# Attention with a gated feed-forward branch on one core: accumulator gating, last additions and row scaling moved from VectorE to GpSimd, and 122 instead of 117 heads computed with V stationary

## The chip, the core and the metric

The kernel runs on one core of one Trainium2 chip. The metric is the device time of one execution in microseconds (us). The kernel before takes 1219.27 us (median of 3 runs, 1219.25 to 1219.4). The profile of one execution spans 1217.5 us from its first to its last instruction, with a granted TensorE clock of 1.000.

Engine names as the profile has them: PE is TensorE (matmuls), PEld its weight loads, DVE is VectorE, ACT is ScalarE, POOL is GpSimd, SP is SyncE, which issues most transfers. PSUM is the memory that matmuls write to, SBUF the working memory.

## What is computed

```python
# B=1, Sq=Sk=2048, D=512, H=32 heads of Dh=128, F=1792; inputs and outputs are bf16
xn = layernorm(x)
q  = (xn @ wq), split into 32 heads
p  = softmax(q @ k_cache^T * Dh**-0.5)          # per head
s  = concat_heads(p @ v_cache) @ wo
h  = relu(xn @ w1 + b1)**2
g  = silu(h @ w2 + b2)
out = x + s * g
```

## The kernel before, in words

**Tiling.** The 2048 query rows are cut into four blocks of 512 (index j), each of four row tiles of 128 (index qt; jt = 4*j + qt counts all 16). For each block the kernel runs over the 32 heads, so g = 32*j + h counts 128 (block, head) pairs, here called heads. Each head has eight steps; a step handles two key tiles of 128. Step numbers pi run from 0 to 1023 and are the clock of the program: the main loop at the end of the kernel emits, for each step, the scores of that step (`gen_scores`: two matmuls of 512 columns into `psA`, then one exponential of 128x1024 by ACT into one of eight `pT` buffers), some matmuls of other work from a job list (`fill_one`: query projections, the two feed-forward products, the output product with `wo`, all into the two banks of `psF`), and, two steps behind, the product with V (`gen_pv`).

**Two forms of the product with V.** In the A form (`gen_pv`) the probabilities are the stationary operand and V with a column of ones the moving one: eight matmuls of 129 columns a step, 64 a head. The ones column delivers the softmax denominator; DVE copies the result out (`o_un`, line 253), takes reciprocals (`rden`), POOL multiplies (`o_bf`), and a transposing transfer writes `oT`. In the B form (`gen_pv_b`) V is stationary and the probabilities move: two matmuls of 512 columns a step, 16 a head. The result is already transposed, ACT copies it to `o_col`, but the denominator has to be summed apart. For each of the eight `pT` tiles of a head, either DVE reduces the tile at once (`den_part`, line 286, `d_part<-pT`), or POOL first adds the two halves (`part_add`, line 239, `h_sum<-pT`) and DVE reduces the half (`part_half`, `d_part<-h_sum`). A few small DVE operations, two trips through memory (`den_sum` to `rec_read`) and one POOL multiplication (`den_scale`, `oT<-o_col,r_all`) follow. `at_a` chooses: heads below `FIRST_B` = 3, the last three, and those in `A_HEADS` = (10, 31, 41, 64, 96) take the A form, eleven in all; 117 take the B form.

**The gate and the output.** `job_o2` makes g: DVE adds the bias b2 to the product (`z_t`), ACT takes tanh of half of it, and DVE forms `g_all` = (tanh + 1) * z, which is twice silu. `job_wo` accumulates s in `acc`, eight heads (a chunk m) at a time, in f32. When all but the last chunk are in (line 1216 on), `acc_gate` multiplies `acc` by 0.5 * g_all on DVE (line 249), and `acc_add` adds x on POOL. When the last chunk comes, DVE multiplies it by 0.5 * g_all straight from PSUM into `tmp_t` (the same memory as `z_t`), adds `acc` into `out_t` (line 239), and the row tile is written out, by a transfer that POOL issues (line 294) or, in the last block, SP. In the last block the additions of row tiles 0 and 2 are POOL's.

**The next block's rows.** While block j runs, `ln_bn`, `ln_rstd` and `ln_next` normalise the x rows of block j+1. `ln_scale`, (x - mean) * rstd on 128x512 in bf16 by DVE (line 245, `xn_t<-x_ln`), is the first part of `ln_next`; a transposing transfer to `xnT` follows.

**What orders the work.** Nothing is scheduled at run time. The program is written out in advance by a planner that keeps for each engine the time at which it expects it to be free (`_cost` has the durations; `_uses_port` names the operations of DVE and POOL that the planner lets not overlap). Urgent work, such as copying a `psF` bank out, is emitted when its job ends. Work that can wait stands in lists: `quiet` for DVE (entered by `calm`, with a due step), `pool_quiet` for POOL, `sync_quiet` for SP. `fill_dve`, `fill_pool` and `fill_sync` take from them what is ready and fits before the expected time of PE plus some room (`ROOM` 800 ns for DVE, `POOL_ROOM` 300 ns for POOL). `fill_pool` also takes a `pT` tile over from DVE as a `part_add`, whenever POOL would be free and DVE's list is worth more than `POOL_OWED` = 3500 ns. So how many of the tiles POOL halves is an outcome of the planner, not a setting. On each engine the order then is fixed, and an instruction that waits holds up all behind it.

Of the kernel before, what the change touches and what calls it, by code (L numbers as in the profile page):

```python
# [5 lines left out]
ACT = mybir.ActivationFunctionType  # L6
# [53 lines left out]
def _cost(name, fn):  # L60
    f, k = fn.func, fn.keywords
    n = _elements(k["out"])
    if name == "PE":
        return n / 2.4 + 2.5, n / 2.4 + 166
    if name == "ACT":
        return n * 0.83 + 70, n * 0.83 + 172
    if name == "POOL":
        if f is _tt and n > 1:
            c = n * 2.3 + 55 if k["out"].tensor.name == "oT" else n * 2.05 + 60
            return c, c + 50  # L70
        return (500, 560) if f is _tt else (n + 100, n + 150)
    if f is _reduce_t:
        n = _elements(k["in_"])
    elif f is _reduce:
        n = _elements(k["in_"]) * 1.3 + 35
    elif f is _recip:
        n = n * 3.1
    elif f in (_bn_stats,):
        n = _elements(k["in_"])
    elif f is _ts and _in_sbuf(k["in0"]):  # L80
        n = n / 2
    return n / 0.96 + 70, n / 0.96 + 150


def _uses_port(name, fn):
    f, k = fn.func, fn.keywords
    if name == "POOL":
        return f in (_tt, _ts)
    if name == "DVE":
        if f in (_tt, _stt):  # L90
            return _in_sbuf(k["in0"]) and _in_sbuf(k["in1"])
        if f in (_ts, _copy):
            return _in_sbuf(k.get("in0", k.get("in_")))
    return False
# [206 lines left out]
def bass_recurrent_scan__mha_block_cached__dense_activation_squared_relu__prompt_kernel(  # L301
# [37 lines left out]
    LATE_EVICT = 250  # L339
    POOL_ROOM = 300  # L340
    SLACK = 1500
    FIRST_B = 3
    A_HEADS = (10, 31, 41, 64, 96)
    POOL_OWED = 3500
    HALF_SLACK = 600
    VW = 136
# [173 lines left out]
        ln_bn(j, i)  # L520
        ln_rstd(j, i)

    def ln_scale(j, i):
        jt = j * TPB + i
        assert jt < TPB or ln_prev(jt) in t_xnr
        t_xn[jt] = E(DV, partial(_ts, out=ln_y(jt), in0=ln_x(jt),
                                 scalar1=mv_t[:, i, 0:1], scalar2=rstd[:, i:i + 1],
                                 op0=ALU.subtract, op1=ALU.mult),
                     deps=[t_xr[jt], t_xnr.get(ln_prev(jt))])
# [7 lines left out]
        assert j < 2 or n_xuse[j - 2] == NFC + H  # L537

    def ln_next(j, i):
        ln_scale(j, i)  # L540
        ln_transpose(j, i)
        if i + 2 < TPB:
            ln_load(j, i + 2)
# [346 lines left out]
    def needs(fn):  # L890
        f, a = fn.func, fn.args
        if f in (den_part, part_half):
            m = b_no[a[0] // NPR]
            if m >= 2 and m - 2 not in t_sum:
                return None
            return [t_exp[a[0]]] if f is den_part else [t_part[a[0]]]
        if f in (den_sum, den_turn, den_write, den_read, den_total, den_recip, rec_write,
                 rec_read, den_scale):
            g = a[0]
            m = b_no[g]  # L900
            if f is den_sum and tiles[g] < NPR:
                return None
            first, before = {
                den_sum: (t_parts.get(g, []), t_row), den_turn: ([t_sum.get(m)], t_dw),
                den_write: ([t_row.get(m)], t_dr), den_read: ([t_dw.get(m)], t_tot),
                den_total: ([t_dr.get(m)], t_rw), den_recip: ([t_tot.get(m)], {}),
                rec_write: ([t_rec.get(m)], t_spr), rec_read: ([t_rw.get(m)], t_scale),
                den_scale: ([t_col.get(m), t_spr.get(m)], {})}[f]
            if m >= 2 and f not in (den_recip, den_scale):
                first = first + [before.get(m - 2)]  # L910
            return first
        if f is norm_recip:
            return t_oev[a[0]]
        if f is norm_scale:
            return [t_rden.get(a_no[a[0]])]
        if f is acc_gate:
            return [t_acc[a[1]], t_g.get(a[0] * TPB + a[1])]
        if f is acc_add:
            jt = a[0] * TPB + a[1]
            return [t_ug.get(jt), tok_xt.get(jt)]  # L920
        if f is ln_bn:
            return [t_xl.get(a[0] * TPB + a[1])]
        if f is ln_rstd:
            return [t_bn.get(a[0] * TPB + a[1])]
        if f is ln_next:
            return [t_xr.get(a[0] * TPB + a[1])]
        return gate_needs[fn]

    def ready_at(fn):
# [217 lines left out]
    def job_o2(j, qt):  # L1147
        jt = j * TPB + qt

        def mm(n, bank):  # L1150
            t = E(PE, partial(_mm, out=bankF(bank), lhsT=h2T[:, n, qt * P:(qt + 1) * P],
                              rhs=w2_sb[:, n, :], start=(n == 0), stop=(n == NFC - 1)),
                  deps=[tok_w2, t_bankF[bank], t_h2[j, n]], inc=(n == NFC - 1))
            if t is not None:
                assert n_w2[0] == NFC // 2
                t_o2[j, qt] = t
                t_o2j.append(jt)

        def evac(bank, step):
            s = jt % 2  # L1160
            assert jt < 1 or jt - 1 in t_g
            tz = E(DV, partial(_tt, out=z_t[:, s, :], in0=bankF(bank), in1=b2bc[:], op=ALU.add),
                   deps=[t_o2[j, qt], tok_b2, t_zrd[s], t_tmp[s]])
            box = [None]

            def gate():
                gs = jt % TPB
                t_g[jt] = t_zrd[s] = t_thr[0] = E(
                    DV, partial(_stt, out=g_all[:, gs, :], in0=th_t[:, 0, :], scalar=1.0,
                                in1=z_t[:, s, :], op0=ALU.add, op1=ALU.mult),  # L1170
                    deps=[box[0], t_fin.get(jt - TPB)])

            def tanh():
                box[0] = E(AC, partial(_act, out=th_t[:, 0, :], in_=z_t[:, s, :], func=ACT.Tanh,
                                       scale=0.5), deps=[tz, t_thr[0]])
                fn = partial(gate)
                gate_needs[fn] = [box[0]]
                calm(step + 8, fn)

            at(step + 1, tanh)  # L1180
            return tz
        return NFC, mm, evac

    t_fin = {}

    def job_wo(j, m, qt, c0=0, c1=D):
        jt = j * TPB + qt
# [15 lines left out]
        def evac(bank, step):  # L1203
# [2 lines left out]
                    t_wodone[j * H + h] = box[0]  # L1206
            place = (bankF(bank) if isinstance(bank, int) else bank[0])[:, 0:c1 - c0]
            if m == 0:
                t_acc[qt] = t = E(DV, partial(_copy, out=acc[:, qt, :], in_=place),
                                  deps=[box[0], t_fin.get(jt - TPB)])  # L1210
            elif not last:
# [1 line left out]
                                              in1=acc[:, qt, :], op=ALU.add),  # L1213
                                  deps=[box[0], t_acc[qt]])
            if m == len(CH[j]) - 2:
                calm(step + 16, partial(acc_gate, j, qt))
                pool_quiet.append(partial(acc_add, j, qt))
            if last:
                s = jt % 2
                assert all(x in t_g for x in t_o2j)  # L1220
                t = E(DV, partial(_stt, out=tmp_t[:, s, c0:c1], in0=place, scalar=0.5,
                                  in1=g_all[:, jt % TPB, c0:c1], op0=ALU.mult,
                                  op1=ALU.mult),
                      deps=[box[0], t_g[jt], t_tmp[s], t_zrd[s]])
                end = jt >= NQB * TPB - 2
                row = (x_t if end else out_t)[:, s, c0:c1]
                eng = GP if j == NQB - 1 and qt in (0, 2) else DV
                t_fin[jt] = t_tmp[s] = E(
                    eng, partial(_tt, out=row, in0=tmp_t[:, s, c0:c1],
                                 in1=acc[:, qt, c0:c1], op=ALU.add),  # L1230
                    deps=[t, t_u[jt], None if end else t_outdma[s]])
                eng, sl = (SP, sl_fin) if j == NQB - 1 else (GP, sl_out)
                dma = S.emit_dma(
                    eng, partial(_dma, out=out[0, jt * P:(jt + 1) * P, c0:c1],
                                 in_=row), sl[s], deps=[t_fin[jt]])
                if c1 == D:
                    t_outdma[s] = dma
            return t
        return nh, mm, evac

    def load_xt(jt):
        if jt < NQB * TPB:
# [3 lines left out]

    def acc_gate(j, qt):
        jt = j * TPB + qt
        t_ug[jt] = E(DV, partial(_stt, out=acc[:, qt, :], in0=acc[:, qt, :], scalar=0.5,
                                 in1=g_all[:, jt % TPB, :], op0=ALU.mult, op1=ALU.mult),  # L1250
                     deps=[t_acc[qt], t_g[jt]])


# [115 lines left out]
                                        in_=bass.AP(tensor=B_b2.tensor, offset=B_b2.offset,  # L1369
                                                    ap=[[0, P], [1, D]])), sl_b2)  # L1370

    at(62, load_b2)
    for i in range(2):
        at(140 + 8 * i, partial(load_xt, i))
    tok_w2 = None
# [14 lines left out]
    for j in range(NQB):  # L1390
        if j + 1 < NQB:
            for i in range(TPB):
# [2 lines left out]
                b = j * SPB + 8 * NPR + 4 * NPR * i  # L1395
                at(b, partial(calm, b + 32, partial(ln_bn, j + 1, i)))
                at(b, partial(calm, b + 32, partial(ln_rstd, j + 1, i)))
                at(b, partial(calm, b + 32, partial(ln_next, j + 1, i)))


    HD = D // 2
# [149 lines left out]
```

The softmax here doesn't subtract the row's maximum and nothing guards it: scores larger than these inputs give would overflow.

## Time and profile before

| | us | share of the span |
|---|---|---|
| span | 1217.5 | |
| PE busy | 1206.4 | 99% |
| ACT busy | 1090.4 | 90% |
| DVE busy | 1067.2 | 88% |
| POOL busy | 1064.2 | 87% |
| POOL `h_sum<-pT`, 758 of 1167 ns | 863.0 | |
| DVE `d_part<-h_sum`, 758 of 678 ns | 495.2 | |
| DVE `d_part<-pT`, 178 of 1213 ns | 215.4 | |
| PE, A form, 704 matmuls | 54.0 | |
| POOL `oT<-o_col,r_all`, 117 of 1284 ns | 150.2 | |

The page names for each group of instructions its line, engine, operation, output and inputs, how many there were, their busy time, the mean ns of one and the idle time of the engine just before them. Most operations are recorded at a shared helper's line (226 is a matmul, 239 an operation on two tensors, 249 one on two tensors and a scalar), so the tile's name tells them apart. A busy PE is no proof that it runs at its peak, since matmuls overlap: the records of two matmuls of 512 columns take 0.59 us together, though the second begins 0.22 us after the first. The distance from the start of one to the start of the next is therefore the measure. Some matmul records are missing from the trace, which shows as a distance of exactly twice the usual.

### The profile page before, as it was taken

How to read it: one execution, taken by the hardware profiler on the slowest of the kernel's cores; microseconds unless marked ns; L12 is line 12 of the kernel's file. 1: busy time of each engine (PE TensorE's matmuls, PEld its weight loads, DVE VectorE, ACT ScalarE, POOL GpSimd, SP SyncE). 2: the span in 40 equal slices, each digit the busy share in tenths (PEclk: the TensorE clock that was granted, in tenths of full speed). 3: DMA queues.
4: the chain of work that ended last, by engine and by line, in shares of the span. 5: the costliest groups of instructions: out<-in, count | busy, mean ns of one | idle time of the engine just before them, and what ended most of it. 6: DMA issues, size and time to landing. Idle time of an engine off the chain costs nothing.

```text
span 1217.5 us, 19712 instructions
## 1 busy us (share of the span) xinstructions
PE 1206.4 (99%) x6150; PEld 668.3 (55%) x6269; DVE 1067.2 (88%) x1865; ACT 1090.4 (90%) x1162; POOL 1064.2 (87%) x982
## 2 busy tenths in 40 slices
PE   9999999999999999999999999999999999999999
PEld 7555555555555555555555555555555555555556
DVE  4798889899999898879999999888999999889973
ACT  7898989999899898999989999999999999989995
POOL 1687999999898899999888899999998889999981
PEclk9999999999999999999999999999999999999999
DMA  9889888888778786777787777877778777677781
GB/s 209 182 202 211 193 181 168 187 170 184 179 157 178 170 161 155 164 159 153 169 167 159 171 167 166 163 163 164 163 163 167 164 164 164 158 160 164 160 156 49
DMA packets 510009, 203.47 MB, mean 167 GB/s; under 512 B 421808, under 2 KB 493744, under 8 KB 509904
## 3 DMA queue, kind: packets, MB, share of 16 engines
q1 hardware_dynamic: 507808, 198.13, 76.2%
q0 software_dynamic: 1424, 3.81, 1.1%
q8 instruction: 50, 0.82, 0.3%
q14 instruction: 55, 0.45, 0.1%
q10 hardware_dynamic: 672, 0.26, 0.1%
HBM read 128.23 MB, written 4.25 MB: 109 GB/s over the span
## 4 chain that ended last, share of the span: by engine, by line
PE 95%; DVE 3%; issue 1%; POOL 1%; ACT 0%; ACTq 0%; POOLq 0%
PE psA L226 36%; PE psO L226 32%; PE psF L226 24%; PE psO L231 3%; DVE d_part L286 1%; DVE acc L249 1%; POOL h_sum L239 0%; ACT pT L235 0%; PE psA L231 0%; DVE qt_sb L253 0%; DVE acc L239 0%; DVE d_sum L282 0%; PE psF L270 0%; POOL oT L239 0%; POOL acc L239 0%
## 5 line engine op out<-in xcount | busy, mean ns | idle before, releaser
L235 ACT ACTIVATE pT<-psA 128x1024 bf16<-128x1024 f32 x1025 | 1036.6, 1025 | 108.2 <-PE psA L226 71.2
L239 POOL TENSOR_TENSOR h_sum<-pT 128x512 f32<-128x512 bf16 x758 | 863.0, 1167 | 63.3 <-DVE d_part L286 31.0
L226 PE MATMUL psA<-qt_sb,kT 128*128 128x512 bf16 x1983 | 594.7, 379 | 3.8 <-ACT pT L235 0.7
L226 PE MATMUL psO<-pT,v_sb 128*128 128x512 bf16 x1832 | 548.1, 379 | 2.0
L286 DVE TRANSPOSE_TENSOR_REDUCE d_part<-h_sum 128x16 f32<-128x512 f32 x758 | 495.2, 678 | 18.1 <-POOL h_sum L239 17.5
L226 PEld LDWEIGHTS psA<-qt_sb,kT 128*128 128x128 bf16 x2032 | 285.5, 144 | 179.2 <-ACT pT L235 4.5
L226 PEld LDWEIGHTS psO<-pT,v_sb 128*128 128x128 bf16 x1872 | 183.2, 98 | 220.0 <-issue 0.6
L286 DVE TRANSPOSE_TENSOR_REDUCE d_part<-pT 128x32 f32<-128x1024 bf16 x178 | 215.4, 1213 | 12.1 <-ACT pT L235 11.4
L226 PE MATMUL psF<-xnT,wq_sb 128*128 128x512 bf16 (+1 forms) x510 | 166.1, 374 | 0.7 <-DVE xnT L253 0.2
L226 PE MATMUL psF<-wo_all,oT 128*128 128x512 bf16 x469 | 160.3, 379 | 0.3
L239 POOL TENSOR_TENSOR oT<-o_col,r_all 128x512 bf16<-128x512 f32 x117 | 150.2, 1284 | 11.6 <-DMA r_all<-r_scr 11.4
L253 DVE CAST qt_sb<-psF 128x512 bf16<-128x512 f32 (+1 forms) x130 | 87.1, 670 | 32.0 <-PE psF L226 28.8
L226 PE MATMUL psF<-xnT,w_sb 128*128 128x512 bf16 x218 | 75.4, 379 | 0.3
L226 PEld LDWEIGHTS psF<-xnT,wq_sb 128*128 128x128 bf16 x520 | 50.3, 98 | 45.9 <-issue 0.3
L226 PE MATMUL psF<-w_sb,h2T 128*128 128x512 bf16 x221 | 73.0, 379 | 0.1
L235 ACT ACTIVATE o_col<-psO 128x512 f32<-128x512 f32 x117 | 69.3, 592 | 0.0
L226 PEld LDWEIGHTS psF<-wo_all,oT 128*128 128x128 bf16 x480 | 46.9, 98 | 40.0
L231 PEld LDWEIGHTS psO<-v_sb,pT 128*128 128x128 bf16 x704 | 46.6, 98 | 19.0 <-ACT pT L235 0.4
L245 DVE TENSOR_SCALAR r_t<-psF,b1f 128x512 bf16<-128x512 f32 x56 | 41.5, 741 | 16.9 <-PE psF L226 15.0
L231 PE MATMUL psO<-v_sb,pT 128*128 128x129 bf16 x704 | 54.0, 220 | 0.1
L282 DVE TENSOR_REDUCE d_sum<-d_part 128x16 f32<-128x144 f32 (+3 forms) x117 | 46.2, 395 | 1.3
L249 DVE SCALAR_TENSOR_TENSOR h2T<-psF,b1f,r_t 128x512 bf16<-128x512 f32 x56 | 41.8, 746 | 1.7
(66 smaller groups left out, 377.4 us busy)
## 6 DMA issues: line engine op xcount, KB each, us to landing
v_sb<-in_A_v_cache_dram SPq DMA_DIRECT2D x508, 128.0 KB, 2.7
r_all<-r_scr SPq DMA_DIRECT2D x117, 256.0 KB, 3.9
wq_sb<-in_A_wq_dram SPq DMA_DIRECT2D x127, 128.0 KB, 3.1
wo_all<-in_A_wo_dram SPq DMA_DIRECT2D x16, 256.0 KB, 3.6
kT<-in_A_k_cache_dram SPq DMA_TRANSPOSE x254, 3.6
w_sb<-in_B_w_dram SPq DMA_DIRECT2D x14, 256.0 KB, 3.7
x_t<-in_A_x_dram POOLq DMA_DIRECT2D x16, 128.0 KB, 2.9
d_scr<-d_row SPq DMA_DIRECT2D x117, 16.0 KB, 2.5
```

The costliest lines, as they stand in the source:

```text
L226: return e.matmul(out, lhsT, rhs, start=start, stop=stop)
L231: return e.matmul(out, lhsT, rhs, start=start, stop=stop, skip_group_check=True)
L235: return e.activation(out, in_, func, bias=bias, scale=scale)
L239: return e.tensor_tensor(out, in0, in1, op)
L245: return e.tensor_scalar(out, in0, scalar1=scalar1, scalar2=scalar2, op0=op0, op1=op1)
L249: return e.scalar_tensor_tensor(out=out, in0=in0, scalar=scalar, in1=in1, op0=op0, op1=op1)
L253: return e.tensor_copy(out, in_)
L282: return e.tensor_reduce(out, in_, axis=AX.X, op=ALU.add)
L286: return e.tensor_reduce(out, in_, axis=AX.X, op=ALU.add, apply_transpose=True)
```

## The change

Six edits that belong together:

1. `acc_gate` becomes a plain product on POOL, from POOL's list.
2. So that the product needs no factor 0.5, the half is put into z: `b2bc` is halved once by POOL at step 66, `z_t` is 0.5 * product + b2bc, tanh loses its scale, and the product of the last chunk with `g_all` loses its 0.5.
3. The last addition becomes `finish`. For the first three blocks it goes to POOL's list, together with the issue of the output transfer; in the last block it is emitted at once, as before, for tiles 0 and 2 on POOL and 1 and 3 on DVE.
4. `ln_scale` of blocks 1 to 3 (12 of the 16) goes to POOL, through POOL's list.
5. `FIRST_B` is 2 and `A_HEADS` holds 64 alone: heads 2, 10, 31, 41 and 96 change from the A form to the B form.
6. The planner is told of the scalar form's cost and port on POOL.

The aim is to take work off DVE, and to use what that frees for the denominators of more heads in the form with V stationary.

```diff
-    FIRST_B = 3
-    A_HEADS = (10, 31, 41, 64, 96)
+    FIRST_B = 2
+    A_HEADS = (64,)
...
     def ln_next(j, i):
-        ln_scale(j, i)
+        ln_scale(j, i, GP)
...
-            tz = E(DV, partial(_tt, out=z_t[:, s, :], in0=bankF(bank), in1=b2bc[:], op=ALU.add),
+            tz = E(DV, partial(_stt, out=z_t[:, s, :], in0=bankF(bank), scalar=0.5, in1=b2bc[:],
+                               op0=ALU.mult, op1=ALU.add),
...
-                box[0] = E(AC, partial(_act, out=th_t[:, 0, :], in_=z_t[:, s, :], func=ACT.Tanh,
-                                       scale=0.5), deps=[tz, t_thr[0]])
+                box[0] = E(AC, partial(_act, out=th_t[:, 0, :], in_=z_t[:, s, :], func=ACT.Tanh),
+                           deps=[tz, t_thr[0]])
...
-                calm(step + 16, partial(acc_gate, j, qt))
+                pool_quiet.append(partial(acc_gate, j, qt))
                 pool_quiet.append(partial(acc_add, j, qt))
...
-                t = E(DV, partial(_stt, out=tmp_t[:, s, c0:c1], in0=place, scalar=0.5,
-                                  in1=g_all[:, jt % TPB, c0:c1], op0=ALU.mult,
-                                  op1=ALU.mult),
+                t = E(DV, partial(_tt, out=tmp_t[:, s, c0:c1], in0=place,
+                                  in1=g_all[:, jt % TPB, c0:c1], op=ALU.mult),
...
-                eng = GP if j == NQB - 1 and qt in (0, 2) else DV
-                t_fin[jt] = t_tmp[s] = E(
-                    eng, partial(_tt, out=row, in0=tmp_t[:, s, c0:c1],
-                                 in1=acc[:, qt, c0:c1], op=ALU.add),
-                    deps=[t, t_u[jt], None if end else t_outdma[s]])
...
+                fn = partial(finish, jt, c0, c1, t)
+                if j == NQB - 1:
+                    finish(jt, c0, c1, t)
+                else:
+                    fin_due.add(jt)
+                    fin_needs[fn] = t
+                    pool_quiet.append(fn)
...
+    def finish(jt, c0, c1, t):
...
+        eng = DV if jt >= NQB * TPB - TPB and s else GP
+        t_fin[jt] = t_tmp[s] = E(
+            eng, partial(_tt, out=row, in0=tmp_t[:, s, c0:c1], in1=acc[:, jt % TPB, c0:c1],
+                         op=ALU.add),
+            deps=[t, t_u[jt], None if end else t_outdma[s]])
...
-        t_ug[jt] = E(DV, partial(_stt, out=acc[:, qt, :], in0=acc[:, qt, :], scalar=0.5,
-                                 in1=g_all[:, jt % TPB, :], op0=ALU.mult, op1=ALU.mult),
+        t_ug[jt] = E(GP, partial(_tt, out=acc[:, qt, :], in0=acc[:, qt, :],
+                                 in1=g_all[:, jt % TPB, :], op=ALU.mult),
...
-                at(b, partial(calm, b + 32, partial(ln_next, j + 1, i)))
+                at(b, partial(pool_quiet.append, partial(ln_next, j + 1, i)))
```

More of the change, by code (lines that the diff above doesn't have):

```diff
@@ L67, in _cost @@
     if name == "POOL":
-        if f is _tt and n > 1:
+        if f in (_tt, _stt) and n > 1:
             c = n * 2.3 + 55 if k["out"].tensor.name == "oT" else n * 2.05 + 60
@@ L87, in _uses_port @@
     if name == "POOL":
-        return f in (_tt, _ts)
+        return f in (_tt, _ts, _stt)
     if name == "DVE":
@@ L521, in ln_stats, with ln_scale @@
         ln_rstd(j, i)
-    def ln_scale(j, i):
+    def ln_scale(j, i, eng=DV):
         jt = j * TPB + i
         assert jt < TPB or ln_prev(jt) in t_xnr
-        t_xn[jt] = E(DV, partial(_ts, out=ln_y(jt), in0=ln_x(jt),
+        t_xn[jt] = E(eng, partial(_ts, out=ln_y(jt), in0=ln_x(jt),
                                  scalar1=mv_t[:, i, 0:1], scalar2=rstd[:, i:i + 1],
@@ L926, in needs @@
             return [t_xr.get(a[0] * TPB + a[1])]
+        if f is finish:
+            jt = a[0]
+            return [fin_needs[fn], t_u.get(jt), t_outdma[jt % 2]]
         return gate_needs[fn]
@@ L1161, in evac @@
             assert jt < 1 or jt - 1 in t_g
-            tz = E(DV, partial(_tt, out=z_t[:, s, :], in0=bankF(bank), in1=b2bc[:], op=ALU.add),
+            assert jt < 2 or not {x for x in fin_due if x % 2 == s}
+            tz = E(DV, partial(_stt, out=z_t[:, s, :], in0=bankF(bank), scalar=0.5, in1=b2bc[:],
+                               op0=ALU.mult, op1=ALU.add),
                    deps=[t_o2[j, qt], tok_b2, t_zrd[s], t_tmp[s]])
@@ L1167, in gate @@
                 gs = jt % TPB
+                assert jt < TPB or jt - TPB in t_fin
                 t_g[jt] = t_zrd[s] = t_thr[0] = E(
@@ L1184, in bass_recurrent_scan__mha_block_cached__dense_activation_squared_relu__prompt_kernel @@
     t_fin = {}
+    fin_due = set()
+    fin_needs = {}
     def job_wo(j, m, qt, c0=0, c1=D):
@@ L1208, in evac @@
             if m == 0:
+                assert jt < TPB or jt - TPB in t_fin
                 t_acc[qt] = t = E(DV, partial(_copy, out=acc[:, qt, :], in_=place),
@@ L1220, in evac @@
                 assert all(x in t_g for x in t_o2j)
-                t = E(DV, partial(_stt, out=tmp_t[:, s, c0:c1], in0=place, scalar=0.5,
-                                  in1=g_all[:, jt % TPB, c0:c1], op0=ALU.mult,
-                                  op1=ALU.mult),
+                assert not {x for x in fin_due if x % 2 == s}
+                t = E(DV, partial(_tt, out=tmp_t[:, s, c0:c1], in0=place,
+                                  in1=g_all[:, jt % TPB, c0:c1], op=ALU.mult),
                       deps=[box[0], t_g[jt], t_tmp[s], t_zrd[s]])
-                end = jt >= NQB * TPB - 2
-                row = (x_t if end else out_t)[:, s, c0:c1]
-                eng = GP if j == NQB - 1 and qt in (0, 2) else DV
-                t_fin[jt] = t_tmp[s] = E(
-                    eng, partial(_tt, out=row, in0=tmp_t[:, s, c0:c1],
-                                 in1=acc[:, qt, c0:c1], op=ALU.add),
-                    deps=[t, t_u[jt], None if end else t_outdma[s]])
[L1232 to L1237, printed above, removed]
+                fn = partial(finish, jt, c0, c1, t)
[5 more added lines that the diff above has]
+                    pool_quiet.append(fn)
             return t
         return nh, mm, evac
+    def finish(jt, c0, c1, t):
+        s = jt % 2
+        end = jt >= NQB * TPB - 2
+        row = (x_t if end else out_t)[:, s, c0:c1]
+        eng = DV if jt >= NQB * TPB - TPB and s else GP
[3 more added lines that the diff above has]
+            deps=[t, t_u[jt], None if end else t_outdma[s]])
+        eng, sl = (SP, sl_fin) if jt >= NQB * TPB - TPB else (GP, sl_out)
+        dma = S.emit_dma(
+            eng, partial(_dma, out=out[0, jt * P:(jt + 1) * P, c0:c1], in_=row), sl[s],
+            deps=[t_fin[jt]])
+        if c1 == D:
+            t_outdma[s] = dma
+        fin_due.discard(jt)
     def load_xt(jt):
@@ L1370, in load_b2, with halve_b2 @@
                                                     ap=[[0, P], [1, D]])), sl_b2)
-    at(62, load_b2)
+    def halve_b2():
+        nonlocal tok_b2
+        tok_b2 = E(GP, partial(_ts, out=b2bc[:], in0=b2bc[:], scalar1=0.5, scalar2=None,
+                               op0=ALU.mult), deps=[tok_b2])
+    at(58, load_b2)
+    at(66, halve_b2)
     for i in range(2):
```

## The prediction

> **What bounds the kernel now.** I read the busy times first, then the chain of work that ended last.
>
> ```profile
> PE 1206.4 (99%) x6150; PEld 668.3 (55%) x6269; DVE 1067.2 (88%) x1865; ACT 1090.4 (90%) x1162; POOL 1064.2 (87%) x982
> ...
> PE 95%; DVE 3%; issue 1%; POOL 1%; ACT 0%; ACTq 0%; POOLq 0%
> ```
>
> PE is busy 99%, and 95% of the chain is PE following PE. Busy is no proof of speed, so I took the distances between starts. In the chain between 284.03 and 291.58 us there are 35 matmuls of 512 columns in 7.55 us: 0.2157 us each, one behind the other. The timeline of PE shows the A form beside it:
>
> ```profile
> 396.14 0.84 PE L231 MATMUL psO<-v_sb,pT 128*128 128x129 bf16 x12
> 396.82 0.60 PE L226 MATMUL psA<-qt_sb,kT 128*128 128x512 bf16 x2
> ...
> 615.13 0.62 PE L231 MATMUL psO<-v_sb,pT 128*128 128x129 bf16 x8
> 616.45 0.38 PE L226 MATMUL psA<-qt_sb,kT 128*128 128x512 bf16 x1 [0.70 <-ACT pT L235]
> ```
>
> Twelve A matmuls take 0.68 us, 0.0567 each. The second pair is the one stall worth the name between 20 and 1200 us: eight such matmuls should end at 615.58, the next begins at 616.45, 0.87 us late. At 610.1 us there may be 0.15 more. So PE is a full pipe, and the change can gain only what it takes off PE's own work, plus this stall.
>
> The chain before 616.45 tells what made it:
>
> ```profile
> 604.68 2.48 DVE acc L249
> 607.17 0.07 issue
> 607.23 1.17 POOL acc L239
> 608.40 0.29 issue
> 608.72 0.56 issue
> 609.28 3.38 POOL h_sum L239 x3
> 612.66 1.23 POOL oT L239
> 613.89 1.12 POOL h_sum L239
> 615.09 1.03 ACT pT L235
> ```
>
> A gating of `acc` on DVE took 2.48 us, POOL stood waiting for it in order, its additions came late, and ACT could not overwrite a `pT` buffer. DVE was already on the chain without a break from 585.91. Last, the waits of the engines beside PE (total, times, longest):
>
> ```profile
> POOL h_sum L239 <- DVE d_part L286: 31.0, 44, 2.0
> POOL out_dram L294 <- DVE out_t L239: 21.2, 12, 2.2
> POOL acc L239 <- DVE acc L249: 8.1, 9, 2.1
> ```
>
> POOL stood 21.2 + 8.1 = 29.3 us behind DVE's last additions and gatings, although it has no more to do with the former than to issue a transfer.
>
> **What the Trainium skill says.** "Perfetto Trace Analysis", Identifying the Most-Contended Engine, calls matmul busy time a poor measure of distance to the roofline; the start distances above agree, 0.59 us of record for two matmuls that occupy 0.43. "SBUF — State Buffer", Who interferes with whom, says that a DVE operation with two SBUF inputs contends with a GpSimd one that reads SBUF, and the loser blocks. The gating has two SBUF inputs, and this trace agrees:
>
> ```profile
> 604.62 2.54 DVE L249 SCALAR_TENSOR_TENSOR acc<-acc,g_all 128x512 f32<-128x512 f32 x1
> 1180.51 0.67 DVE L249 SCALAR_TENSOR_TENSOR acc<-acc,g_all 128x512 f32<-128x512 f32 x1
> ```
>
> The second ran while POOL was idle: 0.67 against a mean of 1.851 us. Some 1.2 us of each gating is waiting for the port, which POOL's row of additions keeps.
>
> **The change, part by part.**
>
> *Heads 2, 10, 31, 41, 96 to the B form, on PE.* A: 64 x 0.0567 = 3.629 us. B: 16 x 0.2157 = 3.451 us. Gain 0.178 a head, 0.9 us in all, on the path. This is sure.
>
> *The same five heads on the others.* Each has 8 tiles. In the present mix (758 of 936 halved by POOL, 81%, 6.48 of 8) a head costs DVE 6.48 x 0.678 + 1.52 x 1.213 = 6.2, plus the four small operations 0.395 + 0.215 + 0.221 + 0.191 = 1.0, less the A form's two copies and a reciprocal (2 x 0.417 + 0.174 = 1.0): 6.2 us. POOL: 6.48 x 1.167 = 7.6, plus 1.284 for the scaling, less 1.037 for the A form's: 7.8 us. ACT: one copy more, 0.592. Five heads: DVE +31, POOL +39, ACT +3. ACT hides its 3 us: a B head asks 8 x 1.025 + 0.59 = 8.8 us of it, and 1217.5 / 128 = 9.5 pass.
>
> *Gating to POOL.* DVE loses 29.6 us (16 x 1.851). POOL has no such row; its addition on the same shapes, also f32 with bf16, takes 1.156: 16 x 1.156 = +18.5.
>
> *Last additions of three blocks to POOL.* DVE loses 12 x 0.735 = 8.8. The one POOL addition of this kind took 1.269: +15.2.
>
> *Row scaling to POOL.* DVE loses 12 x 0.703 = 8.4. POOL's cost is not shown. From above: its rows of one input, 1 column in 0.189 and 128 in 0.552, give 2.86 ns a column, 1.65 us for 512. From below: the skill, "GPSIMD Engine Reference", Elementwise — side-by-side cycle accounting, has 769 ns for 512 elements as a best case. I take 1.2 us, +14.4 (9.2 to 19.8). The planner counts 612 ns, so POOL falls behind its plan by up to 1 us here; the next halvings stand behind it.
>
> *The halves.* One operation on `b2bc`, once, while POOL has gaps (55.4 of 80 us busy from 20 to 100); z and the last product read PSUM before and after, 683 against 690 ns; tanh is the same. Nothing.
>
> *New waits.* `tmp_t` is free for the second next tile only when POOL has finished, and DVE would stand in order behind that with a `psF` bank in hand. Tiles of a chunk are released 15 steps apart, some 17 us, and the buffer is shared by every second: 35 us for a 1.27 us addition. Hidden. Nothing depends soon on the output transfer. In the last block all is as before, so the closing stretch stays.
>
> *Sum.* DVE: +31 - 46.8 = -16. POOL: +39 + 18.5 + 15.2 + 14.4 = +87, with 29 of waits gone. In the ten stretches of 100 us from 100 to 1100 and the one to 1180, POOL's busy time adds to 996 of 1080, DVE's to 979. POOL cannot take 87 more into 84; the planner will hand tiles back to DVE: 40 tiles are 47 us less on POOL and 40 x (1.213 - 0.678) = 21 more on DVE. That leaves POOL near 1036 (96%) and DVE near 984 (91%). It fits, but with less room on POOL than now.
>
> **The forecast** (chance 0.60): the 0.9 us of PE work goes, the stall at 616 goes too, since DVE is no longer held 2 us at a time and POOL no longer waits for it; small slips stay under the room of `pT`'s eight buffers. 1219.27 - 0.89 - 0.87 = 1217.5 us.
>
> **The rivals.**
>
> *The stall stays or moves* (0.20). For: POOL is fuller, the two relieving heads at 31 and 96, where blocks meet, are gone, and there the windows show DVE at 99% (9.90 and 9.88 of 10 us). Against: each block gives DVE back 46.8 / 4 = 12 us, twice what one head costs it. One or two stalls of 0.87 in place of the old one: 1218.4 to 1219.3, say 1218.8.
>
> *POOL becomes the bound* (0.14). The skill, "Perfetto Trace Analysis", Optimizing Scalar/DVE Operations, warns that shifting work between DVE and GpSimd "might not help". For: 96% with an underrated row scaling, and whatever is late on POOL holds an exponential. Against: ACT now waits for POOL only 3.6 us in ten times, and PE passes on just 0.87 of it; what is late is mostly caught. If each of the five heads and each of three block changes had a stall of 0.87, less the one now: 7 x 0.87 = 6.1, less 0.9: 1224.5. With half of that, 1221.9. I put it at 1223.
>
> *More than the sum* (0.06). The opening has waits for transfers and the last exponential holds PE near 1202.9 for about 0.25 us. Were another 1 us to go there, 1216.5. Against: neither stretch is touched but by head 2.
>
> **How the numbers follow.** The forecast's case spreads from 1217.0 to 1218; a little of it and most of the last rival lie below 1216.83 (0.2% under): faster 0.09. Above 1221.71 lies nearly all of the POOL case: slower 0.14. The rest, 0.77, is no change by that measure. The range takes in the forecast, the moved stall and some stalls beyond it, and leaves out the POOL case and half of the last: 1216.8 to 1221.0.
>
> **What would show it.** PE: 384 records of the 129-column form (less the missing ones) and the same 0.216 and 0.057 us. DVE: no gating row, its busy time within 25 us of 1067. POOL: gating at 1.16, additions at 1.27, row scaling between 0.77 and 1.65 us, the two waits on DVE gone, busy above 1095. The 0.87 us gap at block three's start is gone. I am wrong if PE shows new waits for ACT that add up to over 3 us, with POOL `h_sum` released late behind a gating or a scaling, or if fewer than 0.5 us of PE work went.

## The result, and the profile after

The changed kernel takes 1227.57 us (1227.39 to 1227.74), against 1219.26 before on the same chip: a ratio of 1.0068, 95% interval 1.0055 to 1.0081. It is 8.3 us slower, where 1.8 us of gain was forecast, and lies outside the range of 1216.8 to 1221.0.

The page of the changed kernel, busy times and chain that ended last:

```profile
span 1225.4 us, 19463 instructions
...
PE 1214.1 (99%) x6029; PEld 658.5 (54%) x6029; DVE 1078.8 (88%) x1870; ACT 1092.8 (89%) x1167; POOL 1134.7 (93%) x1035
...
PE 69%; POOL 13%; DVE 12%; issue 3%; ACT 1%; DMA 0%; SPq 0%; ACTq 0%; POOLq 0%
```

PE still shows 99%, but it holds 69% of the chain where it held 95%. POOL and DVE hold 25% between them, where they held 4%. POOL's busy share went from 87% to 93%.

The forming of `g_all` in the kernel before, and then the groups of instructions that moved or changed, from the lists of all groups (count, busy us, mean ns, idle time before):

```profile
L249 DVE SCALAR_TENSOR_TENSOR g_all<-th_t,z_t 128x512 bf16<-128x512 bf16 x16 | 16.8, 1047 | 0.0
```

```profile
L249 DVE SCALAR_TENSOR_TENSOR g_all<-th_t,z_t 128x512 bf16<-128x512 bf16 x16 | 30.8, 1926 | 0.0
...
L245 POOL TENSOR_SCALAR xn_t<-x_ln,mv_t,rstd 128x512 bf16<-128x512 bf16 x12 | 24.9, 2079 | 0.0
...
L239 POOL TENSOR_TENSOR acc<-acc,g_all 128x512 f32<-128x512 f32 x16 | 18.4, 1152 | 0.8 <-DVE g_all L249 0.8
...
L239 POOL TENSOR_TENSOR out_t<-z_t,acc 128x512 bf16<-128x512 f32 x13 | 16.5, 1272 | 13.0 <-DVE z_t L239 13.0
```

Gating and last additions cost POOL what was forecast, 1.152 and 1.272 us. Two rows did not come out as planned. The row scaling takes 2.079 us on POOL, above both bounds of the prediction and 1.47 us more than the planner counts. And the forming of `g_all`, which the change left on DVE, went from a mean of 1.047 us to 1.926.

DVE's wait for POOL's halvings in the kernel before, and then the waits of the changed kernel that answer to those shown of before (total, times, longest):

```profile
DVE d_part L286 <- POOL h_sum L239: 17.5, 44, 1.4
```

```profile
DVE d_part L286 <- POOL h_sum L239: 66.8, 138, 2.2
...
POOL h_sum L239 <- DVE d_part L286: 17.8, 17, 2.9
...
POOL out_dram L294 <- POOL out_t L239: 3.3, 11, 0.3
```

POOL's 29.3 us behind DVE's gatings and last additions are gone. The direction has turned: DVE now stands 66.8 us behind POOL's halvings, against 17.5 before.

The distances between starts of matmuls, less 0.216 us (0.057 for the A form), show what PE lost. Fourteen stalls between 190 and 790 us, at 198, 199, 242, 333, 428, 448, 472, 490, 492, 550, 619, 741, 751 and 787 us, add to 9.7 us, where the kernel before had 1.0. That is 8.7 more; less the 0.9 us of matmuls saved it leaves 7.8, and the spans differ by 1225.4 - 1217.5 = 7.9. All of the loss is in these stalls. Five of them, 3.8 us together, end with an exponential of ACT. PE's timeline shows two of the fourteen:

```profile
489.41 0.59 PE L226 MATMUL psA<-qt_sb,kT 128*128 128x512 bf16 x2
491.15 0.38 PE L226 MATMUL psF<-xnT,wq_sb 128*128 128x512 bf16 x1 [1.14 <-DVE z_t L249]
491.37 0.59 PE L226 MATMUL psO<-pT,v_sb 128*128 128x512 bf16 x2
492.63 0.65 PE L226 MATMUL psA<-qt_sb,kT 128*128 128x512 bf16 x2 [0.68 <-ACT pT L235]
```

Two matmuls from 489.41 should end the pair at 489.84; the next starts at 491.15, since DVE came late to empty a `psF` bank. At 492.63 it is ACT that is late: before its exponential, it had to wait for the same DVE operation with the tanh in its queue.

The chain ahead of the longest stall, 1.95 us at 751.4, in order of time, holds both new things:

```profile
729.43 0.71 DVE d_part L286
730.14 4.37 DVE g_all L249
734.51 0.60 DVE qt_sb L253
735.11 1.21 DVE d_part L286 x2
...
742.80 1.14 POOL h_sum L239
743.94 2.03 POOL xn_t L245
745.96 0.00 issue
745.97 1.96 POOL h_sum L239 x2
747.92 0.27 issue
748.20 1.17 POOL h_sum L239
749.36 0.02 issue
749.39 3.56 DVE d_part L286 x4
752.95 0.59 DVE acc L253
```

DVE loses some 3.7 us in one forming of `g_all`. Then POOL falls 1.5 us behind its plan in a row scaling, its halvings come late, DVE waits for the halves in the order fixed in advance, and behind them stands the copy of `acc` that PE needs. The timeline of both engines around the 4.4 us:

```profile
728.24 4.49 POOL L239 TENSOR_TENSOR h_sum<-pT 128x512 f32<-128x512 bf16 x4
...
730.06 4.44 DVE L249 SCALAR_TENSOR_TENSOR g_all<-th_t,z_t 128x512 bf16<-128x512 bf16 x1
732.69 1.27 POOL L239 TENSOR_TENSOR oT<-o_col,r_all 128x512 bf16<-128x512 f32 x1
...
735.87 2.27 POOL L239 TENSOR_TENSOR h_sum<-pT 128x512 f32<-128x512 bf16 x2 [1.92 <-DVE d_part L286]
```

POOL's row ends at 732.69 + 1.27 = 733.96, and DVE's operation at 734.50, 0.54 us later. It waited through several POOL operations, not through one. The row ended because POOL then had to wait 1.92 us for DVE: each halving needs one of three `h_sum` buffers, and DVE empties them.

That a POOL operation follows at once does not always keep DVE out. In the same kernel, 58 us later:

```profile
788.57 2.72 POOL L239 TENSOR_TENSOR h_sum<-pT 128x512 f32<-128x512 bf16 x2
788.62 1.65 DVE L249 SCALAR_TENSOR_TENSOR g_all<-th_t,z_t 128x512 bf16<-128x512 bf16 x1
```

Here DVE got in after the first halving, and the second took 1.60 us in place of 1.16. In the 14 traces of this study, 235 formings of `g_all` or gatings of `acc` on DVE began during a POOL operation that another followed within 0.15 us. 152 of them ended about 0.55 us after that operation (1.78 us at most), and if a halving came next, it took 1.61 us (median). 73 waited until POOL paused (median 2.8 us, longest 4.8) and ended 0.55 us after its last operation; the other ten were hardly delayed, or fit neither. Which of the two it will be is not shown. What is shown is how a long wait ends: of the 68 such operations longer than 1.9 us, 66 ended after POOL had come to an operation that waited for DVE.

### The profile page after: what moved, and what is told of

The parts are those of the page before. It is cut to its first block, busy times and chain, and to the rows that moved or that the text cites. A ratio compares the mean times of both kernels' runs of the same rounds, so it can differ in the third digit from the quotient of the medians.

```text
span 1225.4 us, 19463 instructions
## 1 busy us (share of the span) xinstructions
PE 1214.1 (99%) x6029; PEld 658.5 (54%) x6029; DVE 1078.8 (88%) x1870; ACT 1092.8 (89%) x1167; POOL 1134.7 (93%) x1035
## 4 chain that ended last, share of the span: by engine, by line
PE 69%; POOL 13%; DVE 12%; issue 3%; ACT 1%; DMA 0%; SPq 0%; ACTq 0%; POOLq 0%
PE psA L226 26%; PE psO L226 24%; PE psF L226 18%; POOL h_sum L239 10%; DVE d_part L286 8%; PE psO L231 2%; ACT pT L235 1%; POOL oT L239 1%; DVE g_all L249 1%; POOL acc L239 1%; POOL xn_t L245 1%; DVE qt_sb L253 1%; DVE d_sum L282 1%; DVE h2T L249 0%; DVE r_t L245 0%
## 5 line engine op out<-in xcount | busy, mean ns | idle before, releaser
L239 POOL TENSOR_TENSOR h_sum<-pT 128x512 f32<-128x512 bf16 x775 | 874.4, 1159 | 33.6 <-DVE d_part L286 17.8
L226 PE MATMUL psA<-qt_sb,kT 128*128 128x512 bf16 x2032 | 605.3, 379 | 3.1 <-ACT pT L235 2.9
L226 PE MATMUL psO<-pT,v_sb 128*128 128x512 bf16 x1952 | 580.6, 379 | 0.0
L286 DVE TRANSPOSE_TENSOR_REDUCE d_part<-h_sum 128x16 f32<-128x512 f32 x775 | 517.6, 685 | 69.2 <-POOL h_sum L239 66.8
L226 PEld LDWEIGHTS psO<-pT,v_sb 128*128 128x128 bf16 x1952 | 191.0, 98 | 228.2
L286 DVE TRANSPOSE_TENSOR_REDUCE d_part<-pT 128x32 f32<-128x1024 bf16 x201 | 241.4, 1208 | 6.3 <-ACT pT L235 6.1
L239 POOL TENSOR_TENSOR oT<-o_col,r_all 128x512 bf16<-128x512 f32 x122 | 156.3, 1282 | 12.1 <-DMA r_all<-r_scr 12.0
L282 DVE TENSOR_REDUCE d_sum<-d_part 128x16 f32<-128x144 f32 (+4 forms) x122 | 49.0, 402 | 2.3
L226 PEld LDWEIGHTS psF<-xnT,w_sb 128*128 128x128 bf16 x224 | 21.9, 98 | 19.9 <-DVE acc L239 0.8
L226 PEld LDWEIGHTS psF<-w_sb,h2T 128*128 128x128 bf16 x224 | 21.9, 98 | 19.5
```

The source lines that it names most:

```text
L226: return e.matmul(out, lhsT, rhs, start=start, stop=stop)
L239: return e.tensor_tensor(out, in0, in1, op)
L282: return e.tensor_reduce(out, in_, axis=AX.X, op=ALU.add)
L286: return e.tensor_reduce(out, in_, axis=AX.X, op=ALU.add, apply_transpose=True)
```

## The theories and the experiments

**P, price:** the row scaling is 1.47 us longer than planned, so POOL falls behind its plan twelve times. **S, starvation:** `g_all` on DVE waits for the port until POOL pauses, which takes up to 4.4 us. **L, load:** the five heads, or the moved work as such, are too much for POOL. Each edit makes the planner write out the whole program anew, so a difference of a few tenths of a microsecond between two kernels may be the new order and not the edit. The kernel before was run beside each of the kernels below, and its median was 1219.3 to 1219.4 us every time, so their times can be set against one another.

**1. The row scaling back on VectorE.**

```diff
     def ln_next(j, i):
-        ln_scale(j, i, GP)
+        ln_scale(j, i)
...
-                at(b, partial(pool_quiet.append, partial(ln_next, j + 1, i)))
+                at(b, partial(calm, b + 32, partial(ln_next, j + 1, i)))
```

> The changed kernel with the row scaling of blocks 1 to 3 back on VectorE, all else as changed. Theory P (price): the row scaling takes GpSimd 2.08 us where the planner counts 0.61, and what is queued behind it comes 1.5 us late twelve times; then the stalls just after a scaling (at 472, 490 and 787 us, some 3 to 4 us of the 10) go: 1223.5 to 1225. Theory S (starvation): the gating that makes g_all on VectorE waits for the SBUF port while GpSimd runs operations back to back (means 1.93 us, longest 4.44); that stays, so the stalls after a long gating stay (198, 428, 551, 741, 751: 4 to 5 us). Theory L (load): the five heads alone fill GpSimd; then little changes, 1226 to 1228.

Measured: 1217.89 us, ratio to before 0.9986 (0.9979 to 0.9993). The whole loss is gone, more than any of the three theories asked. The load of the five heads and of the other moves is out as the cause, for they are all still there. The load of the scaling itself, and its place in POOL's list, are not out yet: the edit takes both away (the seventh experiment keeps both). The page of this kernel:

```profile
PE 1210.8 (100%) x6029; PEld 658.9 (54%) x6029; DVE 1078.1 (89%) x1882; ACT 1093.2 (90%) x1167; POOL 1116.3 (92%) x1025
```

POOL is hardly less full (92% against 93%), DVE as full as before, and one stall is left, 0.59 us at 198 us; a forming of `g_all` of 4.71 us stands on the chain ahead of it. The mean forming of `g_all` fell too, from 1.926 to 1.364 us, so this experiment does not separate P from S.

**2. The row scaling on GpSimd, at its true price.**

```diff
+        if f is _ts and n > 256:
+            return n * 3.85 + 110, n * 3.85 + 160
         return (500, 560) if f is _tt else (n + 100, n + 150)
```

> The changed kernel, but the planner is told that a row scaling on GpSimd takes 2.08 us instead of 0.61 (same work on the same engines, in another order). Theory P: the same stalls go as with the scaling on VectorE, 1223 to 1225. Theory L: GpSimd is as full as before, so the time stays at 1226.5 to 1228.5. Theory S: the g_all gatings stay at a mean near 1.9 us and the stalls behind the longest of them stay.

Measured: 1223.1 us, 4.5 less than the changed kernel. Nothing was made faster; only the plan knows the length, and in the new plan POOL takes 766 halvings instead of 775 (busy 1123.9 us instead of 1134.7). That supports P. Of S, the durations hold: `g_all` has a mean of 2.094 us in this kernel. Five stalls are left: 0.58 us at 487, 1.32 at 510, 0.31 at 560, 2.10 at 811 and 1.47 at 934. In the 15 us of chain ahead of the ones at 560 and 811 stands a forming of `g_all` of 4.3 to 4.4 us; ahead of the other three there is none so near, so S does not explain all that is left.

**3. The heads as before.**

```diff
-    FIRST_B = 2
-    A_HEADS = (64,)
+    FIRST_B = 3
+    A_HEADS = (10, 31, 41, 64, 96)
```

> The changed kernel with the heads as before (eleven in the A form), so only the moves to GpSimd and the halves remain. Theory L: the stalls go with the heads: 1219 to 1220.5. Theories P and S: the scaling is as mis-priced as before and GpSimd, with 87 - 39 us more than in the kernel before, still runs in long rows: 1222.5 to 1226.

Measured: 1225.59 us (1.0043, 1.003 to 1.0056). Taking the heads back brings 2.0 of the 8.3 us. Theory L asked for nearly all. The ten executions of this kernel spread from 1222.5 to 1231.0 us, so the 2.0 is rough.

**4. A hand-over of the port.** GpSimd's next operation waits for the forming of `g_all`, in the whole of the changed kernel.

```diff
         if eng is DV and backfill[0] is not None:
             backfill[0](S.ready(deps) + late)
+        if eng is GP and port[0] is not None:
+            deps, port[0] = list(deps) + [port[0]], None
...
                     deps=[box[0], t_fin.get(jt - TPB)])
+                port[0] = t_g[jt]
```

> The changed kernel, with one wait added for each of the sixteen gatings: GpSimd's next operation waits until VectorE's gating into g_all is done, so that VectorE gets the port after at most one GpSimd operation. Theory S: the mean of the gating falls from 1.93 us to 1.2 or less, its longest from 4.44 to under 2, the stalls behind it go (4 to 5 us of 10): 1222 to 1224.5. Theory P: only what follows a scaling counts, so 1226.5 to 1228, or more, since GpSimd loses up to 1 us sixteen times. Theory L: slower than 1227.6 for that reason.

Measured: 1223.35 us, 4.2 less than the changed kernel, although sixteen waits were added. The time is as S said, the durations only in part: the mean fell to 1.662, and single ones still take 3.78 us. POOL can still have operations in its queue that were put there ahead of the hand-over, and DVE can wait for those too: the 3.78 us span three of them.

**5. The row scaling alone, in the kernel before.** The first experiment's edit in reverse, applied to the kernel before (four executions, 1229.4 to 1231.5 us).

> The kernel before with one edit: the row scaling of blocks 1 to 3 on GpSimd through its list, at the planner's 0.61 us. Theory P: the 2.08 us and the 1.5 us of lateness hurt by themselves: 1222 to 1228, with stalls of 0.5 to 2 us behind the scalings. Theory C (they hurt only where the other moves have already filled GpSimd): 1219 to 1221.

Measured: 1230.56 us (1.0092, 1.0077 to 1.0107), 11.3 us slower, 2.6 us beyond the slow end of what P expected. Its groups:

```profile
L249 DVE SCALAR_TENSOR_TENSOR g_all<-th_t,z_t 128x512 bf16<-128x512 bf16 x16 | 30.3, 1894 | 0.0
L249 DVE SCALAR_TENSOR_TENSOR acc<-acc,g_all 128x512 f32<-128x512 f32 x16 | 30.0, 1874 | 0.0
...
L245 POOL TENSOR_SCALAR xn_t<-x_ln,mv_t,rstd 128x512 bf16<-128x512 bf16 x12 | 24.9, 2076 | 0.1
```

The scaling raises `g_all` from 1.047 to 1.894 us by itself, with POOL at 88% of the span, so POOL need not be fuller than before for that. What in POOL's new order does it is not shown. It is not a lack of pauses on the whole: POOL's pauses of 0.15 us or more between 100 and 1180 us add to 75.6 us here and to 80.0 in the kernel before. Nor does it take a wrong price: the mean of `g_all` is highest, 2.094 us, in the second experiment, where the plan knows the length.

**6. The heads alone, in the kernel before.** The edit of the third experiment in reverse, applied to the kernel before.

> The kernel before with the 122 heads and nothing else of the change. The ledger of the prediction says VectorE needs 31 us more and GpSimd 39 us more, with no relief from the moves: VectorE keeps the gatings of acc with their waits for the port, so stalls near 290, 590 and 880 us and 1220 to 1225. If the moves are not needed for the heads, 1218.4 (0.9 us of matmuls gone, nothing else).

Measured: 1221.89 us (1.0021, 1.0013 to 1.0029). The heads do need the moves. Six stalls of 0.49 to 0.65 us are left, at 199, 315, 345, 353, 935 and 973 us. Gatings of `acc` of 2.4 to 2.9 us stand on the chains of those at 315 and 935, 25 and 55 us later than expected, and a forming of `g_all` of 4.71 us on that of the one at 199. The chains of the other three show neither close ahead, and the stall expected near 590 did not come: the time was as expected, the reason only in part.

**7. Both repairs, the scaling still on GpSimd.** The price of the second and the hand-over of the fourth, together.

> The changed kernel with both repairs that leave the row scaling on GpSimd: its price set to 2.08 us and GpSimd's next operation waiting for each gating into g_all. Each alone brought about 4.4 us of the 8.3. If lateness and starvation are separate losses they add: 1218.5 to 1220. If they are one loss (a late GpSimd runs without gaps and so starves VectorE), the second brings little: 1221.5 to 1223. If what is left is the load of the scaling itself (12 x 2.08 = 25 us on GpSimd), it stays above 1220.5.

Measured: 1218.39 us, ratio 0.9992 (0.9983 to 1.0). The repairs add: 4.5 and 4.2 apart, 9.2 together, 0.1 us better than the range for two separate losses. All 25 us of row scaling are still on POOL, from POOL's list, and the loss is gone. Load in all is not quite the same, since the new plan gives POOL 760 halvings (busy 1119.1 us). But POOL's load does not order the times: with 1133.2 us the fourth kernel takes 4.2 us less than the changed one with 1134.7, and the fifth, with 1080.1, is the slowest of all. One stall is left, 0.78 us at 961. The durations of `g_all` (min, median, max):

```profile
L251 DVE SCALAR_TENSOR_TENSOR g_all<-th_t,z_t x16: 647/1176/2114, 116.5 to 1178.2; 128x512 bf16<-128x512 bf16 x16
```

**8. Hand-over, the scaling on VectorE.** The edits of the first and the fourth experiment.

> The changed kernel with the row scaling back on VectorE (1217.9 us) and GpSimd waiting for each gating into g_all. The one stall left there, 0.59 us at 198 us, follows a gating of 4.71 us. Theory S: that gating falls under 2 us, the stall goes, 1217.2 to 1217.5. If the waits added to GpSimd cost more than they bring: 1218 to 1219.

Measured: 1217.21 us, ratio 0.9982 (0.9975 to 0.9989), the fastest kernel of this study and faster than both kernels given. Its durations of `g_all` (min, median, max):

```profile
L249 DVE SCALAR_TENSOR_TENSOR g_all<-th_t,z_t x16: 635/1024/1790, 111.9 to 1177.9; 128x512 bf16<-128x512 bf16 x16
```

The longest was 4.709 us in the first experiment and is 1.790 here. The stall at 198 us has gone and none is left between 30 and 1200 us. The seventh kernel, with the scaling on POOL and rightly planned, is 1.2 us slower; 0.78 of that is its stall at 961, 155 us after the last scaling and behind a row of POOL's halvings, an `oT` and a last addition. So it is not shown that the scaling itself costs 1.2 us.

**9. The moves without the scaling, and with the old heads.** The edits of the first and the third experiment.

> The changed kernel with both the row scaling back on VectorE and the heads as before: what is left is the gating of acc, the last additions and the halves. If the gain of the kernel with the scaling on VectorE (1217.9) is the heads' matmuls (0.9 us) plus the stall at 616 (0.9 us), this one keeps the second alone: 1218.3 to 1218.8. If the moves themselves cost stalls that the heads hide: 1219 or more.

Measured: 1218.99 us, ratio 1.0 (0.9991 to 1.0009). A miss by 0.2 us. The stall at 616 is gone, but a new one of 0.39 us at 779 took nearly half of what that brought.

**10. The scaling alone, at two thirds of its length.** The fifth kernel, with the planner told 1.52 us (`n * 2.75 + 110`).

> The kernel before with the row scaling on GpSimd and the planner told 1.52 us for it instead of 0.61 (it takes 2.08). The lateness falls from 1.47 to 0.56 us, the load stays. Theory P (lateness): from 1230.6 to 1222 to 1225. If the load of 25 us on GpSimd is what costs: 1229 to 1231.

Measured: 1225.29 us (1.0045, 1.003 to 1.006). Of the 11.3 us, 5.3 went by the plan alone. It lies 0.3 us beyond the slow end of what P expected, and well under the range of load. The four executions spread from 1223.3 to 1225.6 us.

**11. The scaling alone, with both repairs.** The fifth kernel with the price of 2.08 us and the hand-over for `g_all` and for the gating of `acc`.

> The kernel before with the row scaling on GpSimd at its true price of 2.08 us, and with GpSimd waiting for each gating on VectorE (of g_all and of acc). If lateness and starvation are all that the scaling costs, it loses nothing: 1218.5 to 1220 against 1230.6 without the two repairs.

Measured: 1221.53 us (1.0016, 1.0009 to 1.0023). The repairs bring 9.0 of the 11.3 us; 2.2 stay, more than expected. In its profile two large stalls are left, 1.17 us at 403 and 1.13 at 616, both in heads of the A form (41 and 64). On the chain of the second stands a gating of `acc` of 2.52 us at 608.7, which waited through two POOL halvings in spite of the hand-over. On the chain of the first there is neither a gating nor a scaling, and its cause stays open.

**12. The kernel before with the hand-over.** For `g_all` and for the gating of `acc`, nothing else.

> The kernel before, with GpSimd waiting for each gating on VectorE (of g_all, mean 1.05 us, and of acc, 1.85 us). Theory S: both means fall to about 1.1 us, the stall at 616 us goes and nothing else does: 1218.3 to 1218.6. If the waits slow GpSimd more than they free VectorE: 1219.3 to 1220.5.

Measured: 1218.32 us, ratio 0.9992 (0.9983 to 1.0), as S expected. No stall is left but the one behind the last exponential. The mean of the gating of `acc` fell from 1.851 to 1.391, less than expected, and `g_all` stayed (1.069). The four gatings of the block with the stall went from 7.8 to 6.5 us together, though one of them still takes 3.1; which of these waits had mattered for the stall is not shown.

The runs in one table, in us:

| heads | gating and additions | scaling | time |
|---|---|---|---|
| 117 | DVE | DVE | 1219.3 (before) |
| 122 | DVE | DVE | 1221.9 |
| 117 | POOL | DVE | 1219.0 |
| 122 | POOL | DVE | 1217.9 |
| 117 | DVE | POOL | 1230.6 |
| 117 | POOL | POOL | 1225.6 |
| 122 | POOL | POOL | 1227.6 (after) |

The eighth combination was not run. With 117 heads the scaling on POOL costs 11.3 us beside gatings on DVE and 6.6 beside gatings on POOL. In the fifth kernel three gatings of `acc` of 2.8 to 3.4 us stand on the chain ahead of a stall of 1.5 us at 607.

## Why the prediction was wrong

**What bounds the kernel, and PE's own gain: right.** The full pipe, 0.2157 and 0.0567 us and the 0.9 us of matmuls stand. With the scaling on VectorE the kernel takes 1217.9, and with the hand-over 1217.2, around the 1217.5 forecast. The stall at 616 was part of the gain: the hand-over alone takes it away and brings 1219.3 to 1218.3.

**Gating and last additions: right.** 1.152 against 1.156 us, 1.272 against 1.269, and POOL's 29 us of waits are gone. DVE's busy time, 1078.8, is within the 25 us given, and POOL's, 1134.7, is above the 1095.

**The share handed back to DVE: too large.** The sum had the planner give 40 tiles back to DVE. At the old mix of 81%, 122 heads would have 790 halvings; the changed kernel has 775, so 15 went back, and POOL is 70 us busier than before, not 40. With the true price in the plan (second experiment) there are 766.

**The term that failed is the row scaling on POOL.** The prediction took 1.2 us with bounds of 0.77 and 1.65; it takes 2.08. The lower bound was the best case that the Trainium skill, "GPSIMD Engine Reference", Elementwise — side-by-side cycle accounting, gives for a tight loop over 512 elements; the measurement decides, and it is 2.7 times that. The upper bound extended a row with one constant (0.552 us for 128 columns). An operation with one constant on 512 columns stands in the profile after, the halving of `b2bc`, with 1.504 us, within that bound. So the row was the wrong form: the scaling has two operations and two scalars read per partition. That these make the 0.57 us between 1.504 and 2.079 was not tested apart.

**The consequence was sized wrongly even for the value taken.** The prediction saw that POOL would fall up to 1 us behind twelve times, and set against it that PE had passed on only one lateness of 0.87 us. That was evidence from one lateness, not from twelve. The tenth experiment comes nearest to the value taken: there the plan is 0.56 us short of each scaling (1.2 us would have been 0.59 too long), and the kernel before still loses 6.0 us. With 1.47 us it loses 11.3.

**The wait that no step had: `g_all` on DVE.** The prediction applied the port to the gating of `acc` alone, which moved away, and did not ask what POOL's rows of operations do to the two-input operation that stays. The Trainium skill, "SBUF — State Buffer", Who interferes with whom, says that the one that issues second blocks while the other holds the port for its whole instruction. The trace agrees in kind, but here DVE blocked through a row of them: 4.44 us, where one POOL operation is 1.15. With GpSimd made to wait for `g_all`, 4.2 of the 8.3 us go, and with the price set right as well, the whole loss.

**The rival was right in kind, wrong in its reason.** The POOL case was priced at 1223, with up to 1224.5, and given 0.14. Its picture of many stalls of about 0.87 us is what happened: fourteen, of 0.69 on average. The sign that the prediction named for being wrong came too: PE's stalls behind ACT add to 3.8 us, over the 3 given. An underrated row scaling was among its reasons. But its cause was to be fullness at 96% in the stretch from 100 to 1180 us. There the seventh and eighth kernels have POOL at 96.2% and 95.5%, without loss, and the changed one at 96.8%; the fifth loses 11 us at 92.6%, where the kernel before has 92.3%.

## What to carry to other kernels

In a program whose order is fixed in advance, a wrong duration in the plan can cost more than the work itself: measure an operation in the form it will have (operations, scalars, types) before it is moved to another engine, or take the bound from that form. When an engine gets fuller, list what else needs the port it holds, and let the filling engine wait for that on purpose: one wait on the filling engine can be cheaper than a row of operations in front of the starved one. And before blaming load, correct the plan and leave the moved work where it is.

## What the runs showed of the hardware

- On GpSimd, an operation with one tensor and two per-partition scalars on 128x512 in bf16 took 2.08 us, one with one tensor and one constant 1.50, and an addition of two bf16 tensors into f32 only 1.16. Two tensor inputs did not make an operation longer than one input did.
- A VectorE operation with two SBUF inputs that takes 0.65 us alone took up to 4.8 us beside GpSimd (third experiment). At the end of a GpSimd operation with the next one following at once, it got in 152 times; 73 times it was passed over and waited until GpSimd paused. It ended about 0.55 us after the GpSimd operation that it had waited for last, in both cases.
- When VectorE got in, GpSimd paid: its next halving took 1.61 us (median of 123) in place of 1.16.
